# Sliding-window attention and a GELU-like MLP on one core: issue order written out by slots, and q and k loaded as contiguous rows

## The chip, the cores and the metric

The kernel runs on one core of a Trainium2 chip. Its engines are TensorE (PE; its weight loads are listed apart as PEld), VectorE (DVE), ScalarE (ACT), GpSimd (POOL) and SyncE (SP); the last two issue the DMAs of this kernel. The metric is device time in microseconds (us); lower is better.

## What is computed

```python
# q, k, v: (8 batches, 8 heads, 576 positions, 64), fp32
scores = scale * np.matmul(q, k.transpose(0, 1, 3, 2))
mask = (rel >= 0) & (rel < window)          # rel = row - column, window 64
...
attn = np.exp(scores)
attn = attn / (np.sum(attn, axis=-1, keepdims=True) + 1e-09)
return np.matmul(attn, v).astype(np.float32)
```

The attention output is laid out as 4608 tokens of 512 values, x, and goes through

```python
h = x @ w_in                                 # 512 -> 2048
g = h * (1.0 / (1.0 + np.exp(-1.702 * h)))
return (g @ w_out).astype(np.float32)        # 2048 -> 512
```

Both kernels compute g as h * (1 + tanh(0.851 h)) and account for the factor 0.5 elsewhere.

## The kernel before

Work is in bf16 with fp32 accumulation. A batch has nine blocks of 64 queries; a block sees a window of 128 keys (its own 64 and the 64 before). Two consecutive blocks make a pair m, of which there are 36; a pair yields 128 tokens. Four pairs make a chunk of 512 tokens; there are nine chunks.

`load_batch` brings in one batch: ten DMAs on GpSimd's queue for the rows of q and k (L184; each partition is a position and gets, for each head, a run of 64 values), five for v (L196), and two on SyncE's queue that copy v into a tile shifted by 64 positions (vA, L200 and L201). TensorE turns q and k: for each pair of heads and each of the two, five transposes into the PSUM tile pst (L218), which ScalarE copies out to qT or kT (L228). A batch has 40 such transposes.

For a pair, 16 score matmuls fill the PSUM tile Spb (L256), ScalarE takes the exponential into E (L264), VectorE multiplies by a mask of zeros and ones into PT (L272), and 16 matmuls with v and a column of ones fill Tacc (L290, called PV below). VectorE takes the reciprocal of the sums (L300) and scales into xs (L302). After four pairs, `flush_transpose_group` turns x: 16 transposes into pxt (L163), copied to xT (L168).

`mlp_chunk` follows for that chunk. Up-projection: for each of 16 slices f of the hidden size, four matmuls into hps (L122), tanh on ScalarE (L130) into th, and (th + 1) * hps on VectorE (L132) into gT_f. PSUM has two hps buffers. Down-projection: for each of four groups of 128 tokens, 16 matmuls into ops (L144, one PSUM buffer), a copy on ScalarE (L152) and a DMA out. w_out is multiplied by 0.5 once after its load (L112).

The order of instructions on each engine is made by a scheduler, which interleaves the pieces as buffers and priorities let it; `tc.high_priority()` puts the loads of the first batches and the weights, and each following batch, ahead of other work.

## Time and profile before

| | us |
|---|---|
| median of 3 runs (lowest, highest) | 434.02 (431.01, 435.81) |
| span of the profiled execution | 429.8 |
| TensorE busy in it | 362.5 |
| ScalarE busy | 178.7 |
| VectorE busy | 174.6 |

The span runs from the first instruction to the last; the time of a run also holds what lies around it. For the profiled execution the page gives the span alone. In the profile, a group row gives line, engine, operation, tiles, shapes and count, then busy time and mean ns of one, then idle time before it and what ended it. A timeline row gives start, duration, engine and line. Matmul ends are modelled and overlap, so the distance between starts tells what a matmul costs. A row of windows gives the stretch and its length, then busy time with the number of instructions for PE, PEld, DVE, ACT and POOL, the granted TensorE clock, the DMA share and GB/s.

### The profile page before, as it was taken

Reading aid. Unit: us, or ns where it says so; the run is one execution under the profiler, and the core shown is the slowest. Engines: PE = TensorE matmul, PEld = TensorE weight load, DVE = VectorE, ACT = ScalarE, POOL = GpSimd, SP = SyncE. Lnnn points to the kernel's source line nnn. Section 1 sums busy time; section 2 is a strip of 40 time slices with the busy share of each in tenths; the row PEclk is TensorE's granted clock in tenths of the full one; section 3 lists DMA queues with packets and bytes.
Section 4 is the critical chain, followed back from the end, with each engine's and each line's share of the span. In section 5 each row is a group of like instructions: output and inputs, shape, how many; then the busy total and the mean of one; then the engine's idle time right before and its main releaser. Section 6 shows DMA issues by size and latency. Waiting matters only on the chain.

```text
span 429.8 us, 6699 instructions
## 1 busy us (share of the span) xinstructions
PE 362.5 (84%) x2768; PEld 178.4 (42%) x2768; DVE 174.6 (41%) x350; ACT 178.7 (42%) x281; POOL 105.7 (25%) x131
## 2 busy tenths in 40 slices
PE   0233894989999999999995999899999999998975
...
DMA  9999999999993999118995083800891010011001
GB/s 92 159 165 136 145 124 152 175 141 119 82 98 60 106 65 104 50 51 52 92 93 85 0 56 53 102 2 18 78 75 43 26 73 2 2 52 47 1 32 66
DMA packets 157438, 33.01 MB, mean 77 GB/s; under 512 B 150240, under 2 KB 152288, under 8 KB 157408
## 3 DMA queue, kind: packets, MB, share of 16 engines
...
q8 instruction: 21, 0.34, 0.4%
...
HBM read 36.70 MB, written 9.44 MB: 107 GB/s over the span
## 4 chain that ended last, share of the span: by engine, by line
PE 65%; DMA 15%; POOL 8%; ACT 5%; DVE 4%; issue 2%; ACTq 0%; POOLq 0%
PE ops L144 28%; PE hps L122 25%; DMA qrows<-in_q_dram 6%; PE Tacc L290 5%; DMA w_out_sb<-in_moe_w_out_dram 4%; PE pst L218 3%; POOL qrows L184 3%; DMA krows<-in_k_dram 2%; POOL vnat L196 2%; DMA out_dram<-o_sb 2%; DVE gT_f L132 2%; POOL krows L184 2%; ACT th L130 2%; PE pxt L163 2%; PE Spb L256 2%
## 5 line engine op out<-in xcount | busy, mean ns | idle before, releaser
L122 PE MATMUL hps<-xT,w_in_sb 128*128 128x512 bf16 x576 | 151.9, 387 | 5.7 <-DVE gT_f L132 4.8
L144 PE MATMUL ops<-w_out_sb,gT_f 128*128 128x512 bf16 x576 | 146.4, 379 | 6.3 <-DVE kT L227 2.1
L132 DVE SCALAR_TENSOR_TENSOR gT_f<-th,hps 128x512 bf16<-128x512 bf16 x144 | 97.7, 684 | 76.8 <-ACT th L130 76.7
L130 ACT ACTIVATE th<-hps 128x512 bf16<-128x512 f32 x144 | 85.3, 600 | 84.9 <-PE hps L122 80.9
L144 PEld LDWEIGHTS <-gT_f 128*128 128x128 bf16 x576 | 54.5, 97 | 69.7 <-issue 5.6
L122 PEld LDWEIGHTS <-w_in_sb 128*128 128x128 bf16 x576 | 50.3, 99 | 55.1 <-issue 10.0
L196 POOL DMA_DIRECT2D vnat<-in_v_dram x40 | 33.9, 886 | 118.6 <-PE Tacc L290 55.1
L152 ACT COPY o_sb<-ops 128x512 f32<-128x512 f32 x36 | 21.1, 587 | 92.7 <-PE ops L144 65.9
L184 POOL DMA_DIRECT2D qrows<-in_q_dram x40 | 34.3, 878 | 68.8 <-PE pst L218 68.0
L264 ACT ACTIVATE E<-Spb 128x1024 bf16<-128x1024 f32 x36 | 37.2, 1032 | 12.4 <-PE Spb L256 11.9
L218 PE MATMUL pst<-ident,qrows 128*128 128x128 bf16 (+1 forms) x160 | 19.8, 239 | 26.6 <-POOL ident L64 15.4
L228 ACT COPY qT<-pst 128x576 bf16<-128x576 bf16 x32 | 20.6, 645 | 45.5 <-PE pst L218 42.9
L184 POOL DMA_DIRECT2D krows<-in_k_dram x40 | 35.5, 937 | 14.6 <-DMA w_in_sb<-in_moe_w_in_dram 7.8
L290 PEld LDWEIGHTS <-PT 128*64 128x64 bf16 x576 | 23.0, 116 | 33.7 <-issue 29.7
L168 DVE COPY xT<-pxt 128x512 bf16<-128x512 bf16 x36 | 15.2, 423 | 51.8 <-PE pxt L163 51.8
L256 PE MATMUL Spb<-qT,kT 64*128 64x64 bf16 x576 | 25.5, 199 | 10.2 <-ACT E L264 6.8
L300 DVE RECIPROCAL rc<-Tacc 128x8 f32<-128x8 f32 x36 | 7.3, 202 | 51.3 <-PE Tacc L290 51.3
L218 PEld LDWEIGHTS <-qrows 128*128 128x128 bf16 (+1 forms) x160 | 13.0, 105 | 35.0 <-DMA qrows<-in_q_dram 15.5
L256 PEld LDWEIGHTS <-kT 64*128 64x128 bf16 x576 | 15.8, 98 | 27.7 <-issue 22.2
L290 PE MATMUL Tacc<-vA,PT 128*64 128x65 bf16 x320 | 21.8, 206 | 6.0 <-DMA vA<-vnat 5.5
L228 ACT COPY kT<-pst 128x576 bf16<-128x576 bf16 x32 | 20.5, 642 | 11.7 <-PE pst L218 11.6
L302 DVE TENSOR_TENSOR xs<-Tacc,rc 128x512 bf16<-128x512 f32 x36 | 24.8, 690 | 1.0
...
## 6 DMA issues: line engine op xcount, KB each, us to landing
...
vA<-vnat SPq DMA_DIRECT2D x8, 325.0 KB, 10.3
...
w_in_sb<-in_moe_w_in_dram POOLq DMA_DIRECT2D x1, 2048.0 KB, 15.3
w_out_sb<-in_moe_w_out_dram POOLq DMA_DIRECT2D x1, 2048.0 KB, 18.1
```

Of the source, the lines that this page charges most:

```text
L122: nc.tensor.matmul(hps[:, :], lhsT=w_in_sb[:, c, f * P : (f + 1) * P], rhs=xT[c][:, tok], start=(c == 0), stop=(c == 3),)
L130: nc.scalar.activation(out=th[:], in_=hps[:], func=AF.Tanh, scale=0.851)
L132: nc.vector.scalar_tensor_tensor(out=gT_f[:], in0=th[:], scalar=1.0, in1=hps[:], op0=ALU.add, op1=ALU.mult,)
L144: nc.tensor.matmul(ops[:, :], lhsT=gT[f][:, tsub * P : (tsub + 1) * P], rhs=w_out_sb[:, f, :], start=(f == 0), stop=(f == 15),)
L184: nc.gpsimd.dma_start(out=rt[0:nrow, j, :, :], in_=src[b, :, P * j : P * j + nrow, :].rearrange("h p d -> p h d"),)
L196: nc.gpsimd.dma_start(out=vnat[0:nrow, i, :, 0:D], in_=v[b, :, P * i : P * i + nrow, :].rearrange("h p d -> p h d"),)
L218: nc.tensor.transpose(out=pst[:, coloff + P * j : coloff + P * j + nrow], in_=rows_t[0:nrow, j, 2 * hp : 2 * hp + 2, :].rearrange("p h d - ...
L228: nc.scalar.copy(out=tt[:, coloff : coloff + S], in_=pst[:, coloff : coloff + S])
L256: nc.tensor.matmul(Spb[:, h % 2, t * 256 + (h // 2) * 64 : t * 256 + (h // 2) * 64 + 64], lhsT=kT[hp][rows, 64 * j : 64 * j + 128], rhs=qT ...
L264: nc.scalar.activation(out=E[:], in_=Spb[:], func=AF.Exp, scale=scale)
L290: nc.tensor.matmul(Tacc[t * 64 : t * 64 + 64, bk, hh * 66 : hh * 66 + 65], lhsT=PT[:].rearrange("p a f -> p (a f)")[:, epos : epos + 64], ...
L302: nc.vector.tensor_tensor(out=xs[:].rearrange("p (b h d) -> p b h d", b=2, h=4), in0=view[:, :, :, 0:D], in1=rc[:].to_broadcast([P, 2, 4, D]),
```

## The change

The scheduler is switched off (`tc.manual_schedule()`): each engine issues in the order of the program text.

**q and k.** A head has 576 rows of 64 values, read as 64 partitions of nine rows each, so a partition gets one contiguous run of 576 values; two heads fill 128 partitions (`load_qk`, two DMAs a batch instead of ten). `spread` copies on VectorE into `wide`, where the two heads lie side by side with zeros in between, four copies a batch. One matmul with `wide` as weights and `sel` (two stacked 64x64 identities) as the moving operand turns one row of the nine for both heads: 72 matmuls a batch, in four units of 16 (`qk_mm`, u = 0 to 3) and one of 8. `qk_out` casts them out of PSUM to every ninth column of `qkt`, q on ScalarE, k on VectorE. In the slots these units use the score tile S.

**v.** Batches 0 and 1 come as fp32 on SyncE's queue into one buffer and are cast (`cast_v`); later ones are loaded as before, and VectorE copies them into the shifted tile (`shift_v`) instead of a DMA.

**MLP.** A slot is one f of one chunk: four up-projection matmuls, tanh and product, whatever attention piece is due in that slot, and four down-projection matmuls of the chunk before. `at` puts TensorE work into a slot and what follows it on other engines at the start of the next; `later` puts other work at a slot's start. From pair 8 on a pair takes four slots: scores of the next pair and PV in the first, the turn of x in the third, where the first unit of a new batch and its `spread` may stand too. The output has two PSUM buffers, and the factor 0.5 is in its copy. x is turned pair by pair. The weights come in four DMAs each. Pairs 0 to 3 and batch 0 come before the slots.

```diff
     psS = ctx.enter_context(tc.tile_pool(name="psS", bufs=1, space=bass.MemoryType.PSUM))
     psT = ctx.enter_context(tc.tile_pool(name="psT", bufs=1, space=bass.MemoryType.PSUM))
-    psM = ctx.enter_context(tc.tile_pool(name="psM", bufs=1, space=bass.MemoryType.PSUM))
     psH = ctx.enter_context(tc.tile_pool(name="psH", bufs=2, space=bass.MemoryType.PSUM))
-    psO = ctx.enter_context(tc.tile_pool(name="psO", bufs=1, space=bass.MemoryType.PSUM))
...
+    psO = ctx.enter_context(tc.tile_pool(name="psO", bufs=2, space=bass.MemoryType.PSUM))
+
+    ctx.enter_context(tc.manual_schedule())
...
+    raw = [[keep.tile([P, 4, RR * D], bf16, name=f"raw_{w}{i}") for w in "qk"] for i in range(2)]
+    wide = [keep.tile([P, 4, RR, 2, D], bf16, name=f"wide_{w}") for w in "qk"]
+    qkt = [keep.tile([P, 8, PAD + S], bf16, name=f"qkt{i}") for i in range(2)]
+    v_nat = [keep.tile([P, 5, H, D + 2], bf16, name=f"v_nat{i}") for i in range(2)]
+    v_off = [keep.tile([P, 5, H, D + 2], bf16, name=f"v_off{i}") for i in range(2)]
+    v_f32 = keep.tile([P, 5, H, D], fp32, name="v_f32")
+    w_in_sb = keep.tile([P, 4, DFF], bf16, name="w_in_sb")
+    w_out_sb = keep.tile([P, 16, DM], bf16, name="w_out_sb")
+    out_tiled = out.rearrange("(n p) d -> p n d", p=P)
...
+    def load_qk(b, hps):
+        for w, src in enumerate((q, k)):
+            nc.gpsimd.dma_start(
+                out=raw[b % 2][w][:, hps, :],
+                in_=src[b].rearrange("(g two) (p r) d -> (two p) g (r d)", two=2, r=RR)[:, hps, :],
+            )
+
+    def spread(b, hps):
+        for w in range(2):
+            for par in range(2):
+                rows = slice(par * 64, par * 64 + 64)
+                nc.vector.tensor_copy(
+                    out=wide[w][rows, hps, :, par, :],
+                    in_=raw[b % 2][w][rows, hps, :].rearrange("p g (r d) -> p g r d", d=D),
+                )
+
+    def load_v_f32(b):
+        for i in range(5):
+            n = P if i < 4 else 64
+            nc.sync.dma_start(
+                out=v_f32[0:n, i, :, :],
+                in_=v[b, :, P * i : P * i + n, :].rearrange("h p d -> p h d"),
+            )
+
+    def cast_v(b):
+        vn, vo = v_nat[b % 2], v_off[b % 2]
+        nc.gpsimd.tensor_copy(out=vn[:, 0:4, :, 0:D], in_=v_f32[:, 0:4, :, :])
+        nc.vector.tensor_copy(out=vo[64:128, :, :, 0:D], in_=v_f32[0:64, :, :, :])
+        nc.vector.tensor_copy(out=vo[0:64, 1:5, :, 0:D], in_=v_f32[64:128, 0:4, :, :])
+
+    def load_v(b):
+        vn = v_nat[b % 2]
+        for i in range(5):
+            n = P if i < 4 else 64
+            nc.gpsimd.dma_start(
+                out=vn[0:n, i, :, 0:D],
+                in_=v[b, :, P * i : P * i + n, :].rearrange("h p d -> p h d"),
+            )
+
+    def shift_v(b):
+        vn, vo = v_nat[b % 2], v_off[b % 2]
+        nc.vector.tensor_copy(out=vo[64:128, :, :, :], in_=vn[0:64, :, :, :])
+        nc.vector.tensor_copy(out=vo[0:64, 1:5, :, :], in_=vn[64:128, 0:4, :, :])
...
+    load_v_f32(0)
+    load_qk(0, slice(0, 2))
+    load_qk(0, slice(2, 4))
+    for t in wide:
+        nc.vector.memset(t[0:64, :, :, 1, :], 0.0)
+        nc.vector.memset(t[64:128, :, :, 0, :], 0.0)
...
+    for j in range(4):
+        load_w_in(j)
...
+    for i in range(2):
+        nc.vector.memset(v_nat[i][:], 1.0)
+        nc.vector.memset(v_off[i][:], 1.0)
+        nc.vector.memset(qkt[i][:, :, 0:PAD], 0.0)
+    masks = {z: build_mask(f"mask_{z}", z) for z in (None, 0, 1)}
...
+    def qk_mm(b, u, ps):
+
+        todo = (
+            [(w, u, r, ps[w], r) for w in range(2) for r in range(8)]
+            if u < 4
+            else [(i % 2, i // 2, 8, ps[0], i) for i in range(8)]
+        )
+        for w, hp, r, dst, col in todo:
+            nc.tensor.matmul(
+                dst[:, col * 64 : col * 64 + 64],
+                lhsT=wide[w][:, hp, r, :, :].rearrange("p two d -> p (two d)"),
+                rhs=sel[:],
+                start=True,
+                stop=True,
+            )
+
+    def qk_out(b, u, ps):
+        dst = qkt[b % 2]
+        if u < 4:
+            for w in range(2):
+                o = dst[:, 2 * u + w, PAD:].rearrange("p (n r) -> p n r", r=RR)[:, :, 0:8]
+                i = ps[w].rearrange("p (r n) -> p n r", r=8)
+                if w == 0:
+                    nc.scalar.copy(out=o, in_=i)
+                else:
+                    nc.vector.tensor_copy(out=o, in_=i)
+        else:
+            o = dst[:, :, PAD:].rearrange("p i (n r) -> p i n r", r=RR)[:, :, :, 8]
+            i = ps[0].rearrange("p (i n) -> p i n", i=8)
+            nc.scalar.copy(out=o, in_=i)
...
+    def scores(m):
+        st = S_of[m] = s_tile()
+        for t, b, j in blocks_of(m):
+            src = qkt[b % 2]
...
+    def x_mm(m):
+        ps = X_of[m] = psT.tile([P, 4, P], bf16, name="pxt", tag="T")
+        xs = xs_of.pop(m)
+        for c in range(4):
+            nc.tensor.transpose(
+                out=ps[:, c, :], in_=xs[:, c * P : (c + 1) * P], identity=ident[:, :]
+            )
+
+    def x_out(m):
+        ch = m // 4
+        if m % 4 == 0:
+            xT[ch] = xt_pool.tile([P, 4, 512], bf16, name="xT", tag="xT")
+        nc.vector.tensor_copy(
+            out=xT[ch][:, :, (m % 4) * P : (m % 4) * P + P], in_=X_of.pop(m)[:]
+        )
...
+    def down_out(ch, tsub):
+        o_sb = ob_pool.tile([P, DM], fp32, name="o_sb", tag="o_sb")
+        nc.scalar.activation(out=o_sb[:], in_=O_of.pop((ch, tsub))[:], func=AF.Copy, scale=0.5)
+        nc.sync.dma_start(out=out_tiled[:, ch * 4 + tsub, :], in_=o_sb[:])
...
+    cast_v(0)
+    load_v_f32(1)
+    load_qk(1, slice(0, 4))
+    for j in range(4):
+        load_w_out(j)
+    for m in range(4):
+        scores(m)
+        exp(m)
+        mask(m)
+        if m > 0:
+            x_mm(m - 1)
+            x_out(m - 1)
+        pv(m)
+        norm(m)
+    x_mm(3)
+    x_out(3)
...
+    def at(slot, f, after=()):
+        pe.setdefault(slot, []).append(f)
+        for g in after:
+            post.setdefault(slot + 1, []).append(g)
+
+    def later(slot, g):
+        post.setdefault(slot, []).append(g)
+
+    def qk_unit(slot, b, u):
+        box = {}
+
+        def mm():
+            s = s_tile()
+            box["p"] = [s[:, 0, :], s[:, 1, :]]
+            qk_mm(b, u, box["p"])
+
+        at(slot, mm, [lambda: qk_out(b, u, box["p"])])
+
+    def period(slot, m, nxt):
+        if nxt is not None:
+            at(slot, lambda: scores(nxt), [lambda: exp(nxt)])
+        at(slot, lambda: pv(m), [lambda: norm(m)])
+        if nxt is not None:
+            later(slot + 2, lambda: mask(nxt))
+        at(slot + 2, lambda: x_mm(m), [lambda: x_out(m)])
+
+    later(0, lambda: spread(1, slice(0, 4)))
+    for u in range(5):
+        qk_unit(u, 1, u)
+    later(2, lambda: cast_v(1))
+    at(5, lambda: scores(4), [lambda: exp(4), lambda: mask(4)])
+    def slot_of(m):
+        return (7, 9, 11, 13)[m - 4] if m < 8 else 4 * (m - 4)
+
+    for m in range(4, NM):
+        period(slot_of(m), m, m + 1 if m + 1 < NM else None)
+
+    free = [s for s in range(14, 16 * NCH) if s % 4 == 2]
+    spare = [s for s in range(14, 16 * NCH) if s % 4 == 3]
+    first = {b: 4 * ((9 * b) // 2 - 5) for b in range(2, B)}
+    plan = {2: [(6, 0), (8, 1), (10, 2), (12, 3), (14, 4)]}
+    for b in range(3, B):
+        last = first[b]
+        slots = [s for s in free if s < last][-4:]
+        plan[b] = [(s, u) for u, s in enumerate(slots)]
+        plan[b].append(([s for s in spare if s < last][-1], 4))
+    for b, todo in plan.items():
+        later(todo[0][0], lambda b=b: spread(b, slice(0, 4)))
+        for s, u in todo:
+            qk_unit(s, b, u)
+        later(slot_of((9 * (b - 1) - 1) // 2) + 1, lambda b=b: load_v(b))
+        later(slot_of(9 * b // 2), lambda b=b: shift_v(b))
+    later(5, lambda: load_qk(2, slice(0, 4)))
+    for b in range(3, B):
+        later(plan[b - 2][-1][0] + 2 if b > 3 else 6, lambda b=b: load_qk(b, slice(0, 4)))
...
+    for ch in range(NCH):
+        for f in range(16):
+            s = 16 * ch + f
+            for g in post.pop(s, []):
+                g()
+            if f % 4 == 0 and f > 0 and ch > 0:
+                down_out(ch - 1, f // 4 - 1)
+            if f == 0 and ch > 1:
+                down_out(ch - 2, 3)
+            up_mm(ch, f)
+            up_act(ch, f)
+            for g in pe.pop(s, []):
+                g()
+            if ch > 0:
+                for i in range(4):
+                    down_mm(ch - 1, f // 4, 4 * (f % 4) + i)
+    down_out(NCH - 2, 3)
+    for tsub in range(4):
+        for f in range(16):
+            down_mm(NCH - 1, tsub, f)
+        down_out(NCH - 1, tsub)
...
```

`up_mm`, `up_act`, `down_mm`, `exp`, `mask`, `pv` and `norm` hold the same operations as before, one f, one quarter or one pair at a time; `pv` alternates between the two blocks of a pair.

Three places show how the order moves. First, VectorE's queue at the start. Before (vnat, vA and kT are tiles of v and k):

```order
L193 MEMSET vnat 128x40
L202 MEMSET vA 64x8x32
L203 MEMSET vA 64x8
L227 MEMSET kT 128x32 x8
L193 MEMSET vnat 128x40
L202 MEMSET vA 64x8x32
L203 MEMSET vA 64x8
L88 COPY mask_N<-band 128x1024 [waits Pool_49]
L88 COPY mask_A<-band 128x1024
L88 COPY mask_B<-band 128x1024
L90 MEMSET mask_A 64x2x128 [waits DVE_49]
L90 MEMSET mask_B 64x2x128 [waits DVE_49]
```

Now, from the sixth instruction on, after four memsets of wide:

```order
L171 MEMSET v_nat_101 128x2640
L172 MEMSET v_off_103 128x2640
L173 MEMSET qkt_99 128x8x32
L171 MEMSET v_nat_102 128x2640
L172 MEMSET v_off_104 128x2640
L173 MEMSET qkt_100 128x8x32
L165 COPY mask_None<-band 128x1024 [waits Pool_49]
L165 COPY mask_150<-band 128x1024
L167 MEMSET mask_150 64x2x128 [waits DVE_49]
L165 COPY mask_153<-band 128x1024
L167 MEMSET mask_153 64x2x128 [waits DVE_49]
L83 COPY wide_q<-raw_q_93 64x18x64 [waits DMASW0_49]
```

Memsets of whole tiles stand ahead of the masks, and only behind these come the first copies that the turning of q and k needs; before, nothing of VectorE's stood ahead of that turning but small memsets.

Second, VectorE's queue between chunk 0 and chunk 1, where batch 3 is spread. L311 is the product of up-projection, L238 the mask, L287 the copy of xT, L202 the cast of k:

```order
L311 SCALAR_TENSOR_TENSOR gT<-th,hps 128x512 [waits Activation_49]
L238 TENSOR_TENSOR PT<-E,mask_150 128x1024
L83 COPY wide_q<-raw_q_95 64x36x64 [waits DMASW0_49]
L83 COPY wide_q<-raw_q_95 64x36x64
L83 COPY wide_k<-raw_k_96 64x36x64 [waits DMASW1_49]
L83 COPY wide_k<-raw_k_96 64x36x64
L311 SCALAR_TENSOR_TENSOR gT<-th,hps 128x512 [waits Activation_49]
L287 COPY xT<-pxt 128x4x128 [waits PE_49]
L202 CAST qkt_100<-S 128x64x8 [waits Activation_49]
```

Four copies stand between two products; they come right behind the mask of the next pair. On TensorE, in that same slot, between the up-projection (L298) and the selector matmuls (L185):

```order
L298 LDWEIGHTS w_in_sb
L298 MATMUL hps<-xT,w_in_sb 128x512
L279 LDWEIGHTS xs [waits DVE_49]
L279 MATMUL pxt<-ident,xs 128x128 [waits PE_49]
L279 LDWEIGHTS xs
L279 MATMUL pxt<-ident,xs 128x128
L279 LDWEIGHTS xs
L279 MATMUL pxt<-ident,xs 128x128
L279 LDWEIGHTS xs
L279 MATMUL pxt<-ident,xs 128x128
L185 LDWEIGHTS wide_q [waits DVE_49]
L185 MATMUL S<-sel,wide_q 128x64 [waits Activation_49]
```

The selector matmuls wait for VectorE (the copies above) and for ScalarE (the score tile S), and the four down-projection matmuls of the slot stand behind them.

Third, up- and down-projection on TensorE. Before, in the middle of the program, behind eight up-projection matmuls:

```order
L122 LDWEIGHTS w_in_sb
L122 MATMUL hps<-xT_125,w_in_sb 128x512
L122 LDWEIGHTS w_in_sb
L122 MATMUL hps<-xT_126,w_in_sb 128x512
L144 LDWEIGHTS gT_f
L144 MATMUL ops<-w_out_sb,gT_f 128x512
L144 LDWEIGHTS gT_f
L144 MATMUL ops<-w_out_sb,gT_f 128x512
L290 LDWEIGHTS PT [waits DVE_49]
L290 MATMUL Tacc<-vA,PT 64x65 [waits PE_49]
L290 LDWEIGHTS PT
L290 MATMUL Tacc<-vA,PT 64x65
```

Now, at the end of one slot and in the next:

```order
L318 LDWEIGHTS gT
L318 MATMUL ops<-w_out_sb,gT 128x512
L318 LDWEIGHTS gT
L318 MATMUL ops<-w_out_sb,gT 128x512
L318 LDWEIGHTS gT
L318 MATMUL ops<-w_out_sb,gT 128x512
L318 LDWEIGHTS gT
L318 MATMUL ops<-w_out_sb,gT 128x512
L298 LDWEIGHTS w_in_sb
L298 MATMUL hps<-xT,w_in_sb 128x512 [waits DVE_49]
L298 LDWEIGHTS w_in_sb
L298 MATMUL hps<-xT,w_in_sb 128x512
```

Up- and down-projection now take turns by fours, the down-projection being that of the chunk before; until now two down matmuls and a few of PV's stood between eights of up-projection, and the rest of the down-projection followed in runs.

325 lines of the change are left out of this document (118 added, 207 removed).

## The prediction

> **What bounds the kernel now.** I read the page first, then the table of windows, then TensorE's own timeline.
>
> ```profile
> span 429.8 us, 6699 instructions
> PE 362.5 (84%) x2768; PEld 178.4 (42%) x2768; DVE 174.6 (41%) x350; ACT 178.7 (42%) x281; POOL 105.7 (25%) x131
> PE   0233894989999999999995999899999999998975
> DMA  9999999999993999118995083800891010011001
> PE 65%; DMA 15%; POOL 8%; ACT 5%; DVE 4%; issue 2%; ACTq 0%; POOLq 0%
> ```
>
> TensorE (PE) holds 65% of the chain; the DMA share of the chain lies where the DMA row shows nines. So there are two regimes. The windows, a line per stretch, put sizes on them:
>
> ```profile
> 0.00:20.00 20.00, 2.44 (x17) 1.69 (x18) 3.06 (x19) 3.19 (x4) 18.89 (x30) 1.00 1.58 119
> 20.00:40.00 20.00, 6.38 (x60) 3.79 (x60) 0.69 (x1) 4.82 (x9) 5.87 (x8) 1.00 1.53 154
> 237.80:278.90 41.10, 39.03 (x312) 19.29 (x312) 19.01 (x40) 20.35 (x33) 4.20 (x5) 1.00 0.55 55
> 394.50:429.80 35.30, 27.85 (x120) 11.46 (x119) 10.19 (x15) 10.70 (x18) 0.00 (x0) 1.00 0.08 30
> ```
>
> In the first 40 us TensorE works 8.8 us. In a middle chunk it works 39.03 of 41.1 us, so only 2.07 us of idle time can be won there; the rest must come from fewer or cheaper matmuls, or from the start and the end. The last stretch idles 7.4 us.
>
> **What a piece of TensorE work costs.** Matmuls are pipelined, so I take the distance from one start to the next:
>
> ```profile
> 54.66 1.06 PE L122 MATMUL hps<-xT,w_in_sb 128*128 128x512 bf16 x2
> 85.75 0.41 PE L256 MATMUL Spb<-qT,kT 64*128 64x64 bf16 x16
> 259.71 0.52 PE L218 MATMUL pst<-ident,krows 128*128 128x128 bf16 x5
> 260.16 1.04 PE L144 MATMUL ops<-w_out_sb,gT_f 128*128 128x512 bf16 x4
> 261.03 0.52 PE L218 MATMUL pst<-ident,qrows 128*128 128x128 bf16 x5
> 306.16 3.63 PE L144 MATMUL ops<-w_out_sb,gT_f 128*128 128x512 bf16 x16
> 309.71 0.35 PE L290 MATMUL Tacc<-vA,PT 128*64 128x65 bf16 x5
> 310.25 0.34 PE L163 MATMUL pxt<-ident,xs 128*128 128x128 bf16 x3
> 322.50 1.90 PE L122 MATMUL hps<-xT,w_in_sb 128*128 128x512 bf16 x8
> 324.24 0.59 PE L144 MATMUL ops<-w_out_sb,gT_f 128*128 128x512 bf16 x2
> ```
>
> Eight up-projection matmuls take 1.74 us (322.50 to 324.24), 0.2175 each; sixteen down ones 3.55, 0.222 each; the 16 PV matmuls that begin at 309.71 take 0.54; five turns of q or k 0.45 (259.71 to 260.16); sixteen scores about 0.5 with their drain; four turns of x about 0.3.
>
> The selector matmul of the change does not exist here: 128x128 weights, 64 moving columns. From below it costs what a PV matmul does, 0.034; from above what a turn does, 0.09. Between them: a turn's five matmuls move 576 columns, which at 0.2175 us per 512 is 0.245 of their 0.45; the other 0.205 is 0.041 per weight load. So 0.027 + 0.041 = 0.068 us, the value I take. A batch needs 72 of them, 4.9 us, with about 5.15 for their five groups, where 40 turns cost 8 x 0.45 = 3.6. The selector form makes TensorE slower by 1.5 us a batch.
>
> **The other engines.** Their mean times (ns behind the comma):
>
> ```profile
> L132 DVE SCALAR_TENSOR_TENSOR gT_f<-th,hps 128x512 bf16<-128x512 bf16 x144 | 97.7, 684 | 76.8 <-ACT th L130 76.7
> L130 ACT ACTIVATE th<-hps 128x512 bf16<-128x512 f32 x144 | 85.3, 600 | 84.9 <-PE hps L122 80.9 <-DVE gT_f L132 3.8
> L264 ACT ACTIVATE E<-Spb 128x1024 bf16<-128x1024 f32 x36 | 37.2, 1032 | 12.4 <-PE Spb L256 11.9
> L302 DVE TENSOR_TENSOR xs<-Tacc,rc 128x512 bf16<-128x512 f32 x36 | 24.8, 690 | 1.0
> L300 DVE RECIPROCAL rc<-Tacc 128x8 f32<-128x8 f32 x36 | 7.3, 202 | 51.3 <-PE Tacc L290 51.3
> L272 DVE TENSOR_TENSOR PT<-E,mask_N 128x1024 bf16<-128x1024 bf16 x28 | 19.3, 689 | 11.4 <-ACT E L264 10.9
> L168 DVE COPY xT<-pxt 128x512 bf16<-128x512 bf16 x36 | 15.2, 423 | 51.8 <-PE pxt L163 51.8
> L152 ACT COPY o_sb<-ops 128x512 f32<-128x512 f32 x36 | 21.1, 587 | 92.7 <-PE ops L144 65.9 <-PE pxt L163 14.1 <-DMA out_dram<-o_sb 10.3
> L218 PEld LDWEIGHTS <-qrows 128*128 128x128 bf16 x128 | 10.0, 107 | 30.5 <-DMA qrows<-in_q_dram 15.1 <-issue 11.3
> L112 DVE TENSOR_SCALAR w_out_sb<-w_out_sb 128x8192 bf16<-128x8192 bf16 x1 | 2.3, 2293 | 1.0 <-DMA w_out_sb<-in_moe_w_out_dram 1.0
> L88 DVE COPY mask_B<-band 128x1024 bf16<-128x1024 bf16 x1 | 0.4, 408 | 0.0
> L88 DVE COPY mask_A<-band 128x1024 bf16<-128x1024 bf16 x1 | 0.8, 789 | 0.0
> L202 DVE MEMSET vA<- 64x256 uint32 x8 | 2.2, 272 | 6.5 <-PE Tacc L290 6.5
> ```
>
> An in-SBUF bf16 copy: 1024 elements in 408 ns and 8192 in 2293 make 0.263 ns an element and 139 ns fixed. One spread copy of 2304 elements is then 0.745 us, four of them 2.98. Its bound from above is the memset's pace, 272/256 = 1.06 ns an element: 2.45 us each, 9.8 for four. The spread's target is strided but its inner 64 elements are dense, as the mask copy's inner runs of its source are, so I take the low end. [...] The casts out of PSUM (512 elements) I price as the 690 ns row on VectorE and the 587 ns row on ScalarE.
>
> **The change, part by part.**
>
> Start, up to the first up-projection, at 54.66 us today. The new VectorE queue has memsets ahead of the first spread: four of 1152 words, four of 2640 elements, two of 256, 15,680 in all, 16.6 us at 1.06; I take 16, and from 1 us on that ends at 17. The masks (five operations, 2.2 us) make 19.2, the first half spread (4 x 0.44) 21. That VectorE is the late one follows from the load: 3.5 MB of q, k and v of batch 0, at the rate of w_in below, need 13 us.
>
> ```profile
> 1.02 0.09 DVE L193 MEMSET vnat<- 128x40 bf16 x1 [1.02 <-PEq L329]
> 15.44 0.74 PE L218 MATMUL pst<-ident,qrows 128*128 128x128 bf16 x5 [15.44 <-POOL ident L64]
> 17.04 0.79 DVE L88 COPY mask_A<-band 128x1024 bf16<-128x1024 bf16 x1
> w_in_sb<-in_moe_w_in_dram POOLq DMA_DIRECT2D x1, 2048.0 KB, 15.3
> ```
>
> (w_in is 4.2 MB at its source: 274 GB/s.) The DMAs: ten loads of q and k a batch become two with rows nine times as long, the two shifts of v on SyncE's queue go, the bytes stay. Up to w_out 15.5 MB are asked for, 57 us at that rate, and w_out is wanted first in slot 16; its scaling by 0.5 (the 2293 ns row) moves into the output copy at no cost. On SyncE's queue v of batch 1 waits for the casts below and holds up only outputs that do not exist yet; at half the rate it lands 9 us later, near 44, before slot 2 wants it. TensorE after idleness pays 0.74 for five turns, 0.15 each; a selector matmul there about 0.11, so a unit of 16 costs 1.8. Then: second unit ends at 24, VectorE's cast behind ScalarE's at 25.6, second half spread 27.4, fourth unit 29.5 with casts to 30.4, two casts of v (between 1.5 and 4.9 us by the two copy paces; I take 2.7) 33.1, first mask 33.8, PV 34.7. Three more pairs follow one after the other, since scores of the next pair stand behind this pair's PV: scores 0.6, drain 0.2, exp 1.03, mask 0.69, xT copy 0.42, PV 0.7, semaphores 0.25, together 3.87 each: 46.3. Norm, turn and copy of the last add 2.2: **48.5** (44 to 54).
>
> Chunk 0, 16 slots without down-projection. The one score buffer S serves a selector unit or a score in each of the first 15 slots. A unit holds it for 1.1 (matmuls) + 0.2 (drain) + 0.6 (ScalarE's cast) + 0.69 (VectorE's cast, which waits for ScalarE's) + 0.1 = 2.7; there are eight of these, 21.6; the two half ones 1.4 each, 2.8; five scores 1.9 each, 9.4. Sum 33.8. On top, the spread of batch 1 (3.0), that of batch 2 (3.7, with the mask ahead of it), the v casts of batch 1 (2.7) and the last xT copy, which now no down matmul covers (3). **46.2** (36 to 58, the high end if TensorE stays as slow as at 54.66, where two matmuls took 1 us).
>
> Chunks 1 to 7, 16 slots each: 64 up and 64 down matmuls 28.1 us; four pairs of scores 0.6, PV 0.64 and turn 0.3 are 6.1; 5 of the 8 selector batches fall here, 5/7 x 5.15 = 3.7. That is 37.9; my same addition for 237.8 to 278.9 gives about 1 us too much, so 37.7, and seven are **264**. VectorE has in each 16 x 0.684 + 4 x (0.69 + 0.89 + 0.42) + 5/7 x (2.98 + 4 x 0.69) + 6/7 x 1.53 (shift of v) = 24.4 us, ScalarE 18: both hide. The output copies hide as well.
>
> But the spread stands in VectorE's queue in the very slot whose first selector unit reads it. Count from the start of the slot two before, which holds scores and PV and lasts 3.0 us; the next lasts 1.75. There up-projection ends at 3.85, tanh at 4.65, the product gT at 5.4; behind it in VectorE's queue the mask ends at 6.1 and the spread at 9.1. TensorE reaches the unit at 5.9, after up-projection and the turn of x; it can begin when the two q copies are done, at 7.6, must wait again for k, and ends at 9.7 where 7.0 would do. 2.7 us, five times, **13.5**; the gT behind the spread comes in time for the up-projection after next. Shifting v costs the PV behind it about 0.5, six times, **3**.
>
> Chunk 8 has no attention: 64 x 0.44 = **28.2**. Then 64 down matmuls, 14.2, with two PSUM buffers and so without the waits between them; from the last copy on as today:
>
> ```profile
> 426.01 0.59 ACT L152 COPY o_sb<-ops 128x512 f32<-128x512 f32 x1 [3.75 <-PE ops L144]
> ```
>
> 429.8 - 426.0 = 3.8, and 0.2 of drain: **18.2**.
>
> Sum: 48.5 + 46.2 + 264 + 13.5 + 3 + 28.2 + 18.2 = 421.6. The median of the runs shown, 434.02, lies 4.2 above the profiled span of 429.8; with the same 4.2 it would be 425.8; the forecast is **426.0 us**, 1.8% faster. Most of the gain lies before chunk 3; the middle chunks trade 41.1 for about 40.
>
> **Rivals.**
>
> *Cheap selector matmuls.* At 0.034 (PV's row; PV also loads full-height weights, but 64 wide) the five batches save 5 x 72 x 0.034 = 12.2 and chunk 0's 144 another 4.9: 409. For it: sixteen scores with 128 wide weights in 0.41.
>
> *The interleaving was there already.* At 324.24 a pair of down matmuls fills in behind the up ones. If a chunk has the same cost as today's less idle time and turns, 41.1 - 2.07 - 3.6 + 3.7 = 39.1, seven cost 9.8 more: 436, no change.
>
> *The spread is slow* (the rival on the other side). Its place is the VectorE queue, in the slots named. At 1.06 ns an element each batch pays 6.8 us more, at seven places 48, and the first half spreads 6: 480 and more. It decides from 1.0 us a batch more, which makes 434: copies of 1.0 us instead of 0.745. For it: mask_A took 789 ns where its like took 408, beside GpSimd's DMA issues. Against it: both other copies. [...]
>
> *Weight loads that hide behind nothing.* At the 107 ns of the weight-load row, 504 selector matmuls cost 0.039 more each, 20: 446. The sixteen scores in 0.41 us speak against it. [...]
>
> **How the numbers follow.** Forecast 0.48, of which 0.13 falls within 1% of before; cheap matmuls 0.20; already interleaved 0.10; slow spread 0.14; bare weight loads 0.08. About 1% is what measurement can tell from no change here. Faster by over 1%: 0.35 + 0.20 = 0.55; within 1%: 0.13 + 0.10 = 0.23; slower: 0.14 + 0.08 = 0.22. The range, 406 to 446, takes in the cheap rival with 3 us to spare, the two at 436 and 446, and the mild form of the slow spread; it leaves out the rest of that one. The forecast's own range is 417 to 434.
>
> **What would show it.** The first up-projection at 48 us, chunk 1's first at 95. Copies of the spread at 745 ns. TensorE waiting 2 to 3 us for the spread once a batch, and nearly nowhere else in chunks 1 to 8. Sixteen selector matmuls in 1.1 us. Consecutive chunks 37 to 41 us apart. Chunk 0 well under 40 us, or waits of TensorE on the tanh product in each slot of a middle chunk, would prove the working wrong.

## The result and the profile after

The changed kernel takes 402.46 us (median of 4 runs, 400.88 to 404.89), the kernel before in the same series 434.9 us (431.01 to 435.81): a ratio of 0.9288, 95% interval 0.9233 to 0.9343. That is 7.1% faster where 1.8% was forecast, and 3.5 us below the lower end of the range.

The top of the page of the changed kernel; the tenths are 40 slices of the span:

```profile
span 399.0 us, 7131 instructions
PE 323.0 (81%) x3024; PEld 167.0 (42%) x3024; DVE 239.9 (60%) x387; ACT 177.9 (45%) x257; POOL 52.4 (13%) x70
PE   0044555766799997996999979997999999999996
DMA  8999989742773332326952302223010000100112
```

TensorE executes 3024 matmuls where it executed 2768, and is busy 39.5 us less (323.0 against 362.5). More matmuls in less time is what this case is about. The stretches cut at first up-projections of chunks (columns: busy time and instructions of PE, PEld, DVE, ACT, POOL, then TensorE's granted clock, DMA share, GB/s):

```profile
0.00:46.55 46.55, 11.82 (x216) 9.64 (x217) 32.80 (x46) 10.15 (x10) 14.10 (x27) 1.00 1.12 186
46.55:399.00 352.45, 311.14 (x2808) 157.33 (x2807) 207.13 (x342) 167.72 (x247) 38.26 (x43) 0.97 0.36 59
171.79:210.18 38.39, 34.49 (x346) 17.81 (x345) 25.07 (x43) 19.98 (x29) 7.25 (x9) 1.00 0.70 105
322.18:353.65 31.47, 31.47 (x257) 15.24 (x256) 17.39 (x32) 14.69 (x23) 0.00 (x0) 1.00 0.09 34
353.65:399.00 45.35, 41.60 (x193) 18.71 (x191) 11.66 (x17) 14.93 (x25) 0.00 (x0) 1.00 0.14 53
```

The start is the first line, chunk 3 the third, chunk 7 (no selector matmuls any more) the fourth, chunk 8 with the tail the fifth. In chunk 7 TensorE does not idle at all.

TensorE's timeline, at the beginning of chunks 0 and 1 and in the middle (start, duration, repetitions; in brackets the idle time before and what ended it):

```profile
46.55 1.87 PE L298 MATMUL hps<-xT,w_in_sb 128*128 128x512 bf16 x4 [0.52 <-DVE xT L287]
95.39 1.02 PE L298 MATMUL hps<-xT,w_in_sb 128*128 128x512 bf16 x4 [3.15 <-DVE xT L287]
188.57 0.41 PE L185 MATMUL S<-sel,wide_q 128*128 128x64 bf16 x8 [1.50 <-DVE wide_q L83]
190.22 0.41 PE L185 MATMUL S<-sel,wide_k 128*128 128x64 bf16 x8 [1.24 <-DVE wide_k L83]
...
198.48 0.39 PE L279 MATMUL pxt<-ident,xs 128*128 128x128 bf16 x4
198.70 0.40 PE L185 MATMUL S<-sel,wide_q 128*128 128x64 bf16 x8
198.93 0.40 PE L185 MATMUL S<-sel,wide_k 128*128 128x64 bf16 x8
199.17 1.03 PE L318 MATMUL ops<-w_out_sb,gT 128*128 128x512 bf16 x4
200.03 1.03 PE L298 MATMUL hps<-xT,w_in_sb 128*128 128x512 bf16 x4
...
201.76 1.03 PE L298 MATMUL hps<-xT,w_in_sb 128*128 128x512 bf16 x4
202.72 0.41 PE L223 MATMUL S<-qkt 64*128 64x64 bf16 x16
203.05 0.22 PE L252 MATMUL Tacc<-v_off,PT 128*64 128x65 bf16 x1
203.06 0.22 PE L252 MATMUL Tacc<-v_nat,PT 128*64 128x65 bf16 x1
...
203.43 1.04 PE L318 MATMUL ops<-w_out_sb,gT 128*128 128x512 bf16 x4
```

Read from start to start: eight selector matmuls 0.23 us, four turns of x 0.22, four big matmuls 0.86 to 0.87, sixteen scores 0.33, sixteen PV matmuls 0.38. Ahead of the scores a gap shows: 201.76 to 202.72 is 0.96, 0.095 more than four up-projection matmuls take. What the steps from scores to PV and from PV to the next matmul cost lies inside the 0.33 and the 0.38. The numbers behind the tile names, 128\*128, 64\*128 and 128\*64, are the rows and columns of a matmul's weights (the weight loads of L223 are listed as 64\*128 64x128, those of L252 as 128\*64 128x64); I call them its form. Scores have 64\*128, PV 128\*64, all else here 128\*128.

The groups of the spread and of the casts out of PSUM, and what TensorE waited for from 95 us on (total, times, longest):

```profile
L83 DVE COPY wide_q<-raw_q 64x2304 bf16<-64x2304 bf16 x14 | 10.5, 751 | 0.1
L83 DVE COPY wide_k<-raw_k 64x2304 bf16<-64x2304 bf16 x14 | 12.4, 886 | 0.4
L200 ACT CAST qkt<-S 128x512 bf16<-128x512 f32 x29 | 17.0, 588 | 47.4 <-PE S L185 46.0
L206 ACT CAST qkt<-S 128x512 bf16<-128x512 f32 x7 | 16.9, 2410 | 0.0
```

```profile
PE S L185 <- DVE wide_q L83: 7.5, 5, 1.5
PE S L185 <- DVE wide_k L83: 5.9, 5, 1.2
PE S L223 <- ACT qkt L206: 4.7, 5, 1.0
```

The first two waits are the forecast stall of the spread. The third was not foreseen: the cast of the fifth unit (L206) takes 2410 ns where its like takes 588, and the next scores wait for it.

### The profile page after: what moved, and what is told of

Its sections match the earlier page's. It is cut to its first block, busy times and chain, and to the rows that moved or that the text cites. A ratio compares the mean times of both kernels' runs of the same rounds, so it can differ in the third digit from the quotient of the medians.

```text
span 399.0 us, 7131 instructions
## 1 busy us (share of the span) xinstructions
PE 323.0 (81%) x3024; PEld 167.0 (42%) x3024; DVE 239.9 (60%) x387; ACT 177.9 (45%) x257; POOL 52.4 (13%) x70
## 4 chain that ended last, share of the span: by engine, by line
PE 66%; DVE 18%; ACT 9%; issue 4%; DMA 2%; POOL 0%; DVEq 0%; ACTq 0%; POOLq 0%
PE ops L318 28%; PE hps L298 25%; ACT qkt L206 4%; PE Tacc L252 4%; DVE wide_k L83 3%; PE S L185 3%; PE S L223 3%; DVE wide_q L83 3%; ACT th L309 3%; DVE gT L311 2%; DMA raw_k<-in_k_dram 2%; DVE PT L238 2%; PE pxt L279 1%; ACT E L233 1%; DVE v_off L113 1%
## 5 line engine op out<-in xcount | busy, mean ns | idle before, releaser
L311 DVE SCALAR_TENSOR_TENSOR gT<-th,hps 128x512 bf16<-128x512 bf16 x144 | 99.1, 688 | 120.6 <-ACT th L309 120.2
L298 PE MATMUL hps<-xT,w_in_sb 128*128 128x512 bf16 x576 | 153.3, 390 | 3.7 <-DVE xT L287 3.7
L318 PE MATMUL ops<-w_out_sb,gT 128*128 128x512 bf16 x576 | 147.2, 383 | 0.0
L298 PEld LDWEIGHTS <-w_in_sb 128*128 128x128 bf16 x576 | 56.5, 100 | 71.0 <-issue 8.9
L318 PEld LDWEIGHTS <-gT 128*128 128x128 bf16 x576 | 52.3, 98 | 55.6 <-issue 1.5
L106 POOL DMA_DIRECT2D v_nat<-in_v_dram x30 | 26.9, 903 | 165.1 <-PE Tacc L252 156.3
L185 PE MATMUL S<-sel,wide_q 128*128 128x64 bf16 x260 | 15.4, 201 | 33.2 <-DVE wide_q L83 30.0
L233 ACT ACTIVATE E<-S 128x1024 bf16<-128x1024 f32 x36 | 36.8, 1023 | 10.7 <-PE S L223 10.6
L200 ACT CAST qkt<-S 128x512 bf16<-128x512 f32 x29 | 17.0, 588 | 47.4 <-PE S L185 46.0
L185 PEld LDWEIGHTS <-wide_q 128*128 128x128 bf16 x288 | 14.8, 106 | 41.3 <-DVE wide_q L83 34.7
L328 ACT ACTIVATE o_sb<-ops 128x512 f32<-128x512 f32 x36 | 23.2, 644 | 18.7 <-PE ops L318 18.7
L223 PE MATMUL S<-qkt 64*128 64x64 bf16 x576 | 15.7, 197 | 12.1 <-ACT qkt L206 9.0
L185 PE MATMUL S<-sel,wide_k 128*128 128x64 bf16 x260 | 15.3, 201 | 9.8 <-DVE wide_k L83 9.8
L202 DVE CAST qkt<-S 128x512 bf16<-128x512 f32 x29 | 19.9, 688 | 4.9 <-ACT qkt L200 4.6
L223 PEld LDWEIGHTS <-qkt 64*128 64x128 bf16 x576 | 11.8, 98 | 25.5 <-issue 19.4
L252 PE MATMUL Tacc<-v_off,PT 128*64 128x65 bf16 x320 | 17.5, 205 | 5.9 <-DVE xT L287 3.2
L238 DVE TENSOR_TENSOR PT<-E,mask_None 128x1024 bf16<-128x1024 bf16 x28 | 19.2, 686 | 2.0 <-ACT E L233 2.0
L185 PEld LDWEIGHTS <-wide_k 128*128 128x128 bf16 x288 | 13.5, 106 | 13.3 <-DVE wide_k L83 11.9
L252 PEld LDWEIGHTS <-PT 128*64 128x64 bf16 x576 | 14.2, 117 | 10.4 <-DVE PT L238 5.1
L206 ACT CAST qkt<-S 128x512 bf16<-128x512 f32 x7 | 16.9, 2410 | 0.0
```

The source lines that it names most:

```text
L106: nc.gpsimd.dma_start(out=vn[0:n, i, :, 0:D], in_=v[b, :, P * i : P * i + n, :].rearrange("h p d -> p h d"),)
L185: nc.tensor.matmul(dst[:, col * 64 : col * 64 + 64], lhsT=wide[w][:, hp, r, :, :].rearrange("p two d -> p (two d)"), rhs=sel[:], start=Tru ...
L206: nc.scalar.copy(out=o, in_=i)
L223: nc.tensor.matmul(st[:, h % 2, t * 256 + hp * 64 : t * 256 + hp * 64 + 64], lhsT=src[rows, 2 * hp + 1, 64 * j : 64 * j + 128], rhs=src[ro ...
L233: nc.scalar.activation(out=E_of[m][:], in_=S_of.pop(m)[:], func=AF.Exp, scale=scale)
L238: nc.vector.tensor_tensor(out=pt[:].rearrange("p a f -> p (a f)"), in0=E_of.pop(m)[:].rearrange("p a f -> p (a f)"), in1=masks[z][:].rearr ...
```

## The experiments

The first four kernels take the change apart; the next four test what the first four suggested; the last four test prices.

**1. PV in the order of before**, in the changed kernel (all eight heads of one block, then of the other, not the blocks in turn):

```
-        for h in range(H):
-            for t, b, j in blocks_of(m):
+        for t, b, j in blocks_of(m):
+            for h in range(H):
```

> The changed kernel with one loop exchanged: the 16 PV matmuls of a pair run through the 8 heads of one block, then through those of the other (as before the change), instead of alternating between the blocks, whose outputs lie on different halves of the partitions. Theory (small matmuls were mis-priced, here because alternating blocks overlap on TensorE): 16 PV matmuls go from 0.38 us back to about 0.54; 28 pairs lie in chunks that TensorE bounds, so 402.5 + 28 x 0.16 = 407, at most 408 with all 36. Rival (PV became cheap because its 16 matmuls stand in one piece, the order within plays no role): 402 to 403 and 0.38 stays.

Measured: 410.92 us (407.43 to 412.53), ratio to before 0.9467 (0.9412 to 0.9522). TensorE's timeline:

```profile
186.84 0.35 PE L252 MATMUL Tacc<-v_nat,PT 128*64 128x65 bf16 x5
...
187.38 1.04 PE L318 MATMUL ops<-w_out_sb,gT 128*128 128x512 bf16 x4
```

Sixteen PV matmuls take 0.54 again, as in before. The two blocks of a pair write different halves of the partitions (rows t\*64 of the accumulator); when they alternate, one starts 0.00 to 0.01 us after the other (203.05 and 203.06 in the changed kernel). The overlap that the theory names shows in these starts, and its size in the rows too: 0.157 us a pair, 5.6 for 36 pairs. The time grew by 8.5, beyond the 408 that the theory gave as its upper end. Part of the other 3 us may be no effect of the order: the granted clock of the profiled execution was 0.969 where the changed kernel had 0.974, some 2 us over such a span (an estimate: 408.5 x 0.031 against 399.0 x 0.026).

**2. The kernel before with a full fifth turn.** Of the five turns of a unit the last had 64 rows; here it has 128, the upper half of which is zeros that nobody reads:

```
-                    if j < 4:
-                        nrow = P
-                        idt = ident[:, :]
-                    else:
-                        nrow = 64
-                        idt = ident[0:64, 0:64]
+                    nrow = P
+                    idt = ident[:, :]
```

> The kernel before, with the fifth turn of q and k made over all 128 rows (the upper 64 set to zero, 128 columns out instead of 64), so that all five turns have one shape; the extra columns are never read. Theory (the 0.45 us of five turns held two changes of shape around the fifth, 64-row turn, not 0.041 us for each weight load): five turns take about 0.28 us, 64 groups save 0.17 each, 11 us of TensorE work, and the time falls to 424 to 430. Rival (each weight load costs 0.041 us that nothing hides): five turns take 0.45 plus 0.03, and the time stays at 434 to 438.

Measured: 435.64 us (434.07 to 439.71), ratio 1.0054 (1.0021 to 1.0086). Two rows of TensorE, and two of its waits from 54 us on:

```profile
279.65 0.45 PE L215 MATMUL pst<-ident,qrows 128*128 128x128 bf16 x5
279.94 0.59 PE L122 MATMUL hps<-xT,w_in_sb 128*128 128x512 bf16 x2
```

```profile
PE ops L144 <- ACT o_sb L152: 16.6, 10, 4.7
PE Tacc L287 <- DMA vA<-vnat: 10.8, 1, 10.8
```

Five turns take 0.29 and not 0.45, although the fifth does twice the rows. The theory's price holds; its total does not, and the rival's total (434 to 438) comes out without the rival's reason. TensorE is busy 5.2 us less behind the first up-projection (336.7 against 341.9), but the scheduler puts the work in another order, in which the output copies are waited for 16.6 us (2.1 in before) and the DMA that shifts v 10.8 (5.5). The granted clock was lower as well, 0.969 against 0.984.

**3. The slots alone**: the changed kernel's order of issue with q, k loaded in blocks of 128 rows and turned by transposes as in before (no spread, no selector, no fifth unit). All else of the change stays, PV's alternation, the two output buffers, the split weight loads and the new way of v too:

```
-        todo = (
-            [(w, u, r, ps[w], r) for w in range(2) for r in range(8)]
-            if u < 4
-            else [(i % 2, i // 2, 8, ps[0], i) for i in range(8)]
-        )
...
+        for w in range(2):
+            for j in range(5):
+                n = P if j < 4 else 64
+                nc.tensor.transpose(
...
```

> The changed kernel with the slots, but with the old way of q and k: ten loads of rows a batch, five transposes for each pair of heads, one copy each out of PSUM (q on ScalarE, k on VectorE), no spread, no fifth unit. Theory (the gain is the order of issue and the packing of small matmuls; the new form of q and k costs its spreads, 2.7 us of wait a batch, and its strided ScalarE cast): TensorE pays 3.6 instead of 2.2 us a batch, but the waits on the spread (six of 2.7 us) and on the strided cast (9 us in all) go, chunk 0 and the start get some 10 us shorter: 370 to 392. Rival (the gain is the contiguous loads and the selector matmuls): 410 or more.

Measured: 371.98 us (371.86 to 372.44), ratio 0.8581 (0.8554 to 0.8609).

**4. The selector form alone**: the kernel before, its scheduler left as it is, with q, k loaded as contiguous rows, spread and turned by selector matmuls:

```
-            for j in range(NB_BLK):
-                nrow = P if j < 4 else 64
-                nc.gpsimd.dma_start(
...
+            nc.gpsimd.dma_start(
+                out=rt[:],
+                in_=src[b].rearrange("(g two) (p r) d -> (two p) g (r d)", two=2, r=9),
+            )
```

> The kernel before with its scheduler, but with the new way of q and k: two contiguous loads a batch, spread on VectorE, selector matmuls, casts into a strided tile (q on ScalarE, k on VectorE). Theory (the order of issue is the gain): 36 units cost TensorE 2.2 instead of 3.6 us a batch, 11 us less in all, of which spreads and single-buffered tiles take back a part: 422 to 434. Rival (the selector form is the gain): 412 or less.

Measured: 426.27 us (425.44 to 427.22), ratio 0.9839 (0.9798 to 0.988).

In both runs the theory holds. The change is two changes of opposite sign. Under the scheduler the selector form gains 7 us (1.6%), although there the first up-projection comes 12.8 us later than in before: behind it TensorE is busy 14.0 us less (327.9 against 341.9), at a granted clock of 1.00 against 0.98:

```profile
67.44:423.40 355.96, 327.89 (x2714) 159.65 (x2712) 189.49 (x340) 160.97 (x241) 25.61 (x31) 1.00 0.48 61
```

In the slots the selector form costs 30.5 us (371.98 to 402.46). Where those 30.5 are, the windows of run 3 tell:

```profile
0.00:38.28 38.28, 13.88 (x185) 9.41 (x186) 23.60 (x33) 7.93 (x9) 26.32 (x38) 1.00 1.61 170
38.28:370.70 332.42, 316.03 (x2584) 157.92 (x2583) 180.39 (x314) 155.13 (x240) 79.95 (x91) 0.98 0.63 69
```

Against the same two lines of the changed kernel: the start is 8.3 us shorter, and behind it TensorE is busy 4.9 us *more* (316.0 against 311.1) but not busy 16.4 us instead of 41.3. The selector matmuls are the cheaper way to turn q and k; their spread, their slow cast and their start cost more than they save.

**5. Small matmuls in pieces.** Run 3, with the 16 scores and 16 PV matmuls of a pair cut into four pieces of 4 + 4 that stand between the up-projection matmuls:

```
         for c in range(4):
+            if between is not None and c > 0:
+                between(c - 1)
```

> The kernel with the slots and the old rows and transposes took 371.98 us. This one is the same program, but from the eighth pair of windows on, the 16 score matmuls and 16 PV matmuls of a pair stand in four pieces of 4 + 4 between the four up-projection matmuls of their slot, not in one piece behind them. Nothing else moves: the same matmuls, the same slot. Theory (the order of before costs time because its scheduler cuts the small matmuls into pieces, and each change of shape on TensorE costs about 0.1 us, as the five turns of before showed: 0.45 us with a 64-row turn among them, 0.28 without): three more changes there and three more back for each of some 28 pairs, about 0.4 to 0.65 us a pair, so 382 to 394 us. Rival (only the number of matmuls and the waits for other engines count, not how small ones are grouped): 371 to 374 us.

Measured: 408.92 us (405.31 to 410.69), ratio 0.9394 (0.9315 to 0.9473). TensorE in run 3, and then in this one, from the first up-projection matmul of a slot to what follows the pair:

```profile
162.37 1.03 PE L269 MATMUL hps<-xT,w_in_sb 128*128 128x512 bf16 x4
163.33 0.41 PE L194 MATMUL S<-qkt 64*128 64x64 bf16 x16
...
164.04 1.04 PE L289 MATMUL ops<-w_out_sb,gT 128*128 128x512 bf16 x4
```

```profile
206.29 0.38 PE L279 MATMUL hps<-xT,w_in_sb 128*128 128x512 bf16 x1
206.60 0.23 PE L198 MATMUL S<-qkt 64*128 64x64 bf16 x4
...
208.61 0.23 PE L198 MATMUL S<-qkt 64*128 64x64 bf16 x4
...
208.96 1.04 PE L299 MATMUL ops<-w_out_sb,gT 128*128 128x512 bf16 x4
```

The same 36 matmuls take 1.67 us in one piece and 2.67 in four. A pair has three changes of form in one piece (to 64\*128, to 128\*64, back) and twelve in four: nine more for 1.0 us, 0.11 each. The direction is the theory's, the size about twice what it said: it had counted the change to the scores and back, not the one between scores and PV. 28 pairs make 28 us of the 37. The other 9 are not the pieces' own: the wait for v's shift is 5.8 us in total here and 0.8 in run 3, and the granted clock was 0.971 against 0.984, some 6 us (an estimate: 409.0 x 0.029 against 370.7 x 0.016).

**6. Down-projection not mixed in.** Run 3, each chunk's 64 down matmuls behind its 16 slots:

```
-            if ch > 0:
-                for i in range(4):
-                    down_mm(ch - 1, f // 4, 4 * (f % 4) + i)
...
+        for tsub in range(4):
+            for f in range(16):
+                down_mm(ch, tsub, f)
+            down_out(ch, tsub)
```

> The kernel with the slots and the old rows and transposes took 371.98 us. This one is the same, but a chunk's 64 down-projection matmuls stand behind its 16 slots, not four in each slot one chunk later. Theory (the slots gain because TensorE always has the other projection's matmuls to issue while ScalarE and VectorE finish a slot's tanh and product): without the down matmuls in a slot, a slot with no attention lasts as long as tanh and product of one f, about 1.1 to 1.2 us against 0.87 us of matmuls, and the last product of a chunk is waited for before its down matmuls: some 3 us a chunk and about 5 more in the last, so about 398 us (390 to 402). Rival (mixing the two projections was already there in before, or is worth nothing here): 368 to 376 us.

Measured: 384.82 us (384.75 to 386.82), ratio 0.8878 (0.8828 to 0.8927). The time lies between the two forecasts: the mixing is worth 12.8 us, half of what the theory gave it. The new wait is the one it named, but shorter:

```profile
PE hps L269 <- DVE gT L282: 7.2, 21, 0.5
```

**7. The spread ahead of time.** The changed kernel; for the last five batches the four spread copies stand one to a slot in the four slots ahead:

```
-        later(todo[0][0], lambda b=b: spread(b, slice(0, 4)))
...
+            for i in range(4):
+                later(todo[0][0] - 4 + i, lambda b=b, i=i: spread_one(b, i // 2, i % 2))
```

> The changed kernel took 402.46 us. This one is the same, but from the fourth block of rows on (b of 3 and more), the four copies that spread the raw rows are issued one in each of the four slots ahead of the batch, not all four in front of its first selector matmuls. Theory (TensorE's wait of 1.50 + 1.24 = 2.74 us at the first selector matmuls of each batch is the four copies standing in one row on VectorE, and nothing else): the five later waits of 2.74 us go, some of it comes back as later products in those slots, so 386 to 392 us. Rival (VectorE is the limit in those slots, so its 2.9 us of copies are waited for wherever they stand, now behind the products): 398 to 403 us.

Measured: 386.6 us (385.11 to 388.2), ratio 0.8908 (0.8854 to 0.8962). What is left of the waits for the spread from 100 us on:

```profile
PE S L192 <- DVE wide_q L90: 2.4, 4, 0.7
```

The theory holds: 13.4 us of waits became 2.4, and 15.9 us came off the time.

**8. The slow cast on VectorE.** The changed kernel, with L206 on the other engine:

```
-            nc.scalar.copy(out=o, in_=i)
+            nc.vector.tensor_copy(out=o, in_=i)
```

> The changed kernel took 402.46 us. This one is the same, but the cast of the fifth unit, whose single elements stand 18 bytes apart in the target, is on VectorE and not on ScalarE, where it took 2410 ns. Theory (the price is ScalarE's own for single elements apart, VectorE writes them at its usual rate of 0.6 to 0.7 us for 512 columns): the waits of scores behind this cast, about 9 us of TensorE's idle time, go, so 392 to 395 us. Rival (the stride costs VectorE as much as ScalarE, some 2.4 us each): the waits stay, now with products behind them, 402 to 408 us.

Measured: 409.65 us (407.22 to 410.75), ratio 0.9431 (0.9372 to 0.9489).

```profile
L206 DVE CAST qkt<-S 128x512 bf16<-128x512 f32 x7 | 16.8, 2395 | 0.0
```

The rival holds, and the time even lies above its 408: VectorE needs 2395 ns for it where ScalarE needs 2410, and is the busier engine (239.9 us against 177.9 in the changed kernel), so the wait of the scores for this cast rises from 4.7 to 8.4 us. The price goes with the place that is written, single 2-byte elements 18 bytes apart, and not with the engine. Nor does it go with the place that is read: the fifth unit reads PSUM in runs of 64 elements, its cheap likes (588 ns on ScalarE, 688 on VectorE) read single ones 256 bytes apart.

**9. Each selector matmul twice**, in the changed kernel:

```
         for w, hp, r, dst, col in todo:
+            for _ in range(2):
-            nc.tensor.matmul(
+                nc.tensor.matmul(
...
```

> The changed kernel took 402.46 us. This one is the same, but each selector matmul is issued twice into the same place (the second writes the same values): 72 more matmuls of 64 columns, each with 128 columns of weights to load, in each of eight batches, 576 in all. Theory (a selector matmul costs 0.029 us, as the rows of eight in 0.23 us show, because its weight load is hidden behind the matmuls before it): 576 times 0.029 us is 17 us, some of it inside the waits for the spread copies, so 412 to 421 us. First rival (0.068 us each, as the prediction had it; the rows of 0.23 us leave out a part of it): 39 us more, 430 to 442 us. Second rival (they stand in idle time and cost nothing): 401 to 406 us.

Measured: 414.38 us (414.1 to 415.65), ratio 0.9542 (0.9499 to 0.9585).

```profile
207.19 0.63 PE L186 MATMUL S<-sel,wide_q 128*128 128x64 bf16 x16
207.66 0.63 PE L186 MATMUL S<-sel,wide_k 128*128 128x64 bf16 x16
208.13 1.03 PE L319 MATMUL ops<-w_out_sb,gT 128*128 128x512 bf16 x4
```

Sixteen take 0.47, 0.029 each, as eight did in 0.23. 576 more cost 11.9 us, 0.021 each, as the theory had it; that the rest falls into waits was not measured apart. The 0.068 of the prediction would have cost 39 us and is excluded.

**10. Run 3 with a full fifth turn**, the edit of run 2 in a kernel that issues in slots:

```
-                n = P if j < 4 else 64
...
-                    identity=ident[0:n, 0:n],
+                    identity=ident[:, :],
```

> The kernel with the slots and the old rows and transposes took 371.98 us. This one is the same, but the fifth turn of each five takes all 128 rows (the upper 64, filled with zeros once, land behind the columns in use), so that no 64-row turn stands between 128-row ones: by the earlier run 0.28 instead of 0.45 us for five. In before that brought nothing (435.64 us). Theory (with the slots TensorE has work at nearly every moment, so time taken from its instructions now comes off the end): 0.17 us times 2 sides times 4 units times 7 batches is 9.5 us, and less in the first one, so 360 to 365 us. Rival (TensorE is not what limits this kernel either, the time goes to another wait as in before): 369 to 374 us.

Measured: 365.19 us (364.57 to 365.61), ratio 0.8407 (0.8364 to 0.8451), the fastest kernel of this study.

```profile
155.21 0.44 PE L169 MATMUL S<-ident,raw_q 128*128 128x128 bf16 x5
155.49 0.44 PE L169 MATMUL S<-ident,raw_k 128*128 128x128 bf16 x5
```

0.28 for five, as in run 2, but here 6.8 us come off the end, which leaves the time 0.2 above the theory's range: in before the scheduler gave the time to other waits (16.6 us for output copies and 10.8 for the shift of v in run 2), in the slots TensorE is busy 306.3 of the 325.8 us behind the first up-projection and sets most of the time.

**11. Fewer elements set ahead of the loop.** Run 7, with only those elements of v's buffers set to 1.0 that no transfer fills:

```
-        nc.vector.memset(v_nat[i][:], 1.0)
-        nc.vector.memset(v_off[i][:], 1.0)
+        for t in (v_nat[i], v_off[i]):
+            nc.vector.memset(t[:, :, :, D : D + 2], 1.0)
+        nc.vector.memset(v_nat[i][64:128, 4, :, :], 1.0)
+        nc.vector.memset(v_off[i][0:64, 0, :, :], 1.0)
```

> The changed kernel with the spread copies issued one to a slot took 386.6 us. This one is the same, but of v's four buffers only the columns and rows that no transfer fills are set to 1.0 ahead of the loop, not all of the 128 x 2640 elements (2.26 us each, with a gap of 0.5 between). Theory (the first spread copy begins at 19.26 us because VectorE is still busy with what is set ahead of it, not because the rows arrive late): some 8 us of that go, the first up-projection starts near 39 us and the kernel takes 377 to 381 us. Rival (the rows arrive just as late, or the transfers that follow are then the limit): 384 to 388 us.

Measured: 381.11 us (380.39 to 382.49), ratio 0.8774 (0.8732 to 0.8816). The first selector matmul of the changed kernel, and of this one:

```profile
20.18 0.61 PE L185 MATMUL S<-sel,wide_q 128*128 128x64 bf16 x8 [20.18 <-DVE wide_q L83]
```

```profile
12.14 0.61 PE L194 MATMUL S<-sel,wide_q 128*128 128x64 bf16 x8 [12.14 <-DVE wide_q L83]
```

It comes 8.0 us earlier, so VectorE's memsets were what held it. The first up-projection comes at 40.23, 7.7 earlier than in run 7 (47.91), and 5.5 reach the end: the theory, at the edge of its interval.

**12. The slow cast in two halves**, one on each engine, added to run 11:

```
-            nc.scalar.copy(out=o, in_=i)
+            nc.scalar.copy(out=o[:, 0:4], in_=i[:, 0:4])
+            nc.vector.tensor_copy(out=o[:, 4:8], in_=i[:, 4:8])
```

> This one is the kernel with the light setting of v's buffers and the spread copies one to a slot, and beside that the cast of the fifth unit (single elements 18 bytes apart, 2410 ns on ScalarE, 2395 ns on VectorE) is cut into two halves, one on each engine. Theory (the engines pay by the element that is written apart, so each half takes about 1.2 us, and the wait of scores behind it, about 0.95 us a batch, goes with it): 5 to 7 us less than the kernel without the cut, or 370 to 376 us if that one takes 379. Rival (the halves get in each other's way, or the two engines' other work is pushed back by as much): no less than the kernel without the cut, within 2 us.

Measured: 382.91 us (382.3 to 383.4), ratio 0.8811 (0.8773 to 0.885): no gain.

```profile
L215 ACT CAST qkt<-S 128x256 bf16<-128x256 f32 x7 | 9.0, 1292 | 1.1 <-PE S L194 1.1
L216 DVE CAST qkt<-S 128x256 bf16<-128x256 f32 x7 | 9.0, 1279 | 4.3 <-ACT qkt L215 4.3
```

Each half costs about half, 1292 and 1279 ns against 2410 and 2395 for the whole, so here the engines do pay by the element. But VectorE's half waits until ScalarE's is done, so the two take 2.57 us one behind the other. Why it waits the runs do not show; both halves read one PSUM buffer and write one tile.

## Why the prediction was right in direction and wrong in size

**What held.** The first up-projection was put at 48.5 and came at 46.55; chunk 0 at 46.2 and took 48.8; chunk 1 at 94.7 and began at 95.39. VectorE's queue of memsets, masks and the first spread was indeed what the start waited for: the first spread copy was put at 19.2 and came at 19.26, and run 11 shows the cause. In the 3.87 us put for a pair ahead of the slots, the 0.2 for drain and the 0.25 for semaphores are the author's estimates, without a row; measured are 3.37 from scores to scores (34.22 and 37.59), with 0.04 to 0.06 us from the end of one step's row to the start of the next (exponential, mask and PV begin at 31.83, 32.89 and 33.64, the rows before them end at 31.79, 32.85 and 33.58). The stall of the spread was put at 2.7 us five times; the rows say 1.50 + 1.24, and run 7 took it away. Chunk 8 and the tail were put at 46.4 and took 45.35; the median was put 4.2 above the profiled span and lies 3.5 above it.

Chunk 0 came near in part by luck. Its mechanism held: where nothing else is waited for, a selector unit and a score pass the one buffer S every 4.96 us (units begin at 75.83, 80.83, 85.79 and 90.75), and 2.7 + 1.9 was forecast. But a unit's matmuls, priced at 1.1, take 0.47 to 0.83 there, and against that stand the slow cast of the fifth unit and a granted clock of 0.86 in this stretch, where TensorE's rows show half speed at times (1.89 us for four up-projection matmuls at 53.79, 1.03 at 51.40).

**What failed** is one step, the prices in "What a piece of TensorE work costs", and through them the term **264** for chunks 1 to 7. With 13.5 for the spread and 3 for v's shift it made 280.5; measured are 258.3 (95.39 to 353.65). The 22 us of the miss stand there:

| term, chunks 1 to 7 | price predicted | measured | difference |
|---|---|---|---|
| selector matmuls of a batch, 5 batches | 5.15 | 72 x 0.029 = 2.1 | -15.3 |
| scores and PV of a pair, 28 pairs | 1.24 | 0.33 + 0.38 + 0.11 for gaps = 0.82 | -11.8 |
| turn of x, 28 | 0.3 | 0.22 | -2.2 |
| big matmuls of a chunk, 7 | 28.1 | 32 fours x 0.865 = 27.7 | -2.8 |
| v's shift, in all | 3 | 0.6 | -2.4 |
| wait for the cast L206, in all | 0 | 4.7 | +4.7 |

These sum to -29.8, 8 more than the miss. Of these 8, 1.4 are the rounding of the 264 and about 3 the granted clock, which was 0.96 in two of the chunks (an estimate: 0.04 of 38.9 and of 39.4); the last 3 are not assigned.

The selector's price came from this sentence: "a turn's five matmuls move 576 columns, which at 0.2175 us per 512 is 0.245 of their 0.45; the other 0.205 is 0.041 per weight load." The other 0.205 was no weight load. Runs 2 and 10 show 0.28 for five turns with the same five weight loads, so 0.17 of it came from the 64-row turn between 128-row ones, two changes of form. Its own lower bound, 0.034 from PV's row, was too high as well: run 9 measures 0.029, and PV with alternating halves takes 0.38 for sixteen, 0.024 each. The price of PV came from a row in block order, 0.54, which run 1 gives again, and the sum took 0.64 for it. The price of scores came from a row behind which TensorE waits, so that its length had to be guessed: about 0.5, and 0.6 in the sum. Elsewhere in before sixteen scores in one piece take 0.34 (from 131.89 to 132.23). So 0.16 of the 0.42 a pair is the order in PV, and the rest is allowance that the rows do not bear out.

What the rows of runs 2, 5 and 10 share is the change of form: 0.17 us for two in the five turns of runs 2 and 10, 1.0 for nine in run 5, about 0.1 us each. Counted in the traces from the first up-projection on, with TensorE's busy time from the windows of the same stretch:

| kernel | changes of form | TensorE busy, us | not busy, us |
|---|---|---|---|
| before | 356 | 341.9 | 33.3 |
| before, full fifth turn (2) | 246 | 336.7 | 44.3 |
| before, selector form (4) | 238 | 327.9 | 28.1 |
| slots alone (3) | 209 | 316.0 | 16.4 |
| slots, full fifth turn (10) | 97 | 306.3 | 19.5 |
| the changed kernel | 97 | 311.1 | 41.3 |

From run 3 to run 10, 112 fewer changes give 9.7 us, 0.087 each, although 56 fifth turns became twice as wide; run 5 gives 0.11. From before to the changed kernel there are 259 fewer, 23 us at 0.09; the order in PV is 5.6 us by the rows of run 1; together about 29 of the 30.8 us of busy time that went. The granted clocks of these executions differ (0.984 in before, 0.974 in the changed kernel), some 3.5 us by the estimate used above, so the sum is rough. Behind the first up-projection, then, the gain came from work put together in forms and not from idle time, of which there is even 8 us more; the start is 8.1 shorter. The cause could be seen in part before: the prediction counted 576 columns for five turns, so it knew of the 64-row one, and read its cost as the cost of weight loads.

**The rivals.** "Cheap selector matmuls" (409) was the nearest, and right on its point; that scores and PV too were priced too high was missing in it. "The interleaving was there already" falls: run 6 gives the mixing 12.8 us. Run 3 takes 61 off without the selector form, but that is more than the order of issue: PV's alternation is in it, and its other parts (two output buffers, split weight loads, the new way of v) were not tested one by one. The "slow spread" did not come, in its mild form neither: a copy takes 0.74 to 0.85 us, against the 1.0 from which it was to decide. The mean of 886 ns for k holds a single slow one, the second of these two k copies, which alone takes 2.34 us while GpSimd casts v; the two q copies just ahead took 1.53 together:

```profile
47.98 3.12 DVE L83 COPY wide_k<-raw_k 64x2304 bf16<-64x2304 bf16 x2
48.38 2.11 POOL L98 CAST v_nat<-v_f 128x2048 bf16<-128x2048 f32 x1 [20.45 <-DMA v_f<-in_v_dram]
```

"Weight loads that hide behind nothing" falls with run 9.

**What was not priced.** The prediction gave all casts 0.59 and 0.69 us. The fifth unit writes single elements 18 bytes apart and took 4.1 times as long on ScalarE (2410 ns against 588) and 3.5 times on VectorE (2395 against 688); that its target is not dense could be read in the diff. No run varies the distance, so why such elements cost this much is not shown. The runs of 8 elements (L200) pay nothing that shows, 588 against 587 ns for the dense fp32 output copy in before.

**Still open:** the 3 us of the table that no row accounts for, how the 61 us of run 3 divide among its parts beyond what runs 1, 5 and 6 show, and why VectorE's half of the cast waits in run 12.
